# Chunks of 512 tokens in place of 384 in an attention + feed-forward kernel, with part of the second weight fetched from DRAM for each chunk

## Chip, cores and metric

One core of a Trainium2 chip. The time is device microseconds, the median of three runs: 662.34 us before (661.67 to 663.45).

## What is computed

Attention of 4 sequences of 768 tokens with 8 heads of 64. A query sees the keys within 16 tokens, and one summary per block of 32 tokens (maximum of its keys, mean of its values, log 32 added to its score). The output, 3072 tokens of 512, goes through two products with a gate between them, all in fp32:

```python
k_sum = k.reshape(B, H, nb, block, D).max(axis=3)
v_sum = v.reshape(B, H, nb, block, D).mean(axis=3)
mask_l = np.abs(pos[:, None] - pos[None, :]) < window
scores_all = concatenate([where(mask_l, scores_l, -1e9), scores_s + log(block)])
x = softmax(scores_all) @ concatenate([v, v_sum])      # 3072 x 512
h = x @ w_in                                           # 512 x 2048
sp = np.maximum(h, 0.0) + np.log1p(np.exp(-np.abs(h)))
g = h * erf(sp)
out = g @ w_out                                        # 2048 x 512
```

The weights come as 64-bit floats.

## The kernel before

**Chunks and periods.** The 3072 tokens are cut into NCH = 8 chunks of T = 384 (half a sequence each). For each chunk the 2048 inner columns are taken in NG = 4 groups of 512; a chunk's group is a *period* k, 32 in all. A *quad* is the attention of one chunk for two heads; a chunk has four, 32 in all, numbered so that quads 0 to 3 belong to the first chunk. The steady loop does one quad's attention in each period, a chunk ahead.

**First product** (`mm1`, L535 to L547). Weights and x are each split in two fp32r parts, high and low, and three products of parts are added: for each of four column tiles f (128 inner columns), 4 x 3 matmuls of 128 x 384 into one PSUM bank, `h0` or `h1` in turn. `hout` (L549) then reads the bank twice: ACT's tanh into `wt`, DVE's (early on also ACT's) copy into `hc`. `wt` and `hc` have three buffers each. `logs` and `erfs` (L564, L570) finish the gate on ACT; tanh and erf are in one table set, ln and exp in the other, and a table load (L780) is issued at each change. `gsplit` (L575) multiplies and splits on DVE.

**Second product** (`mm2`, L597) of period k-1 runs in period k: four tiles i times three token tiles t, accumulated over a chunk's four periods in banks `o0` to `o2`. For the first chunk it is plain fp32 on the unsplit weights (L605), later three fp32r matmuls of 512 columns (L609). `evac` (L618) copies the banks out at the end of a chunk.

**Attention.** `scores` (L419) into the double bank `pa`; `softmax` (L454) adds the mask (L457), takes the maximum (L465) and divides (L482) on DVE, exponentials on ACT one window at a time (L470); `transp` (L484) turns the result through `pa`, ACT copies it; `av` (L500) writes the output into a bank of its own, `px`; `xsplit` (L515) splits it into the parts xh and xl (L525). k, v and q windows come by DMA (`load_quad`, `load_quad_v`), their tiles single-buffered. `load_nat` and `summaries` (L324, L334) make a new sequence's summaries, starting four quads before its first chunk; `summaries_turn` transposes them through `px`.

**Weights.** Sixteen units of 1 MB, `load_w` (L237), in the order of `order` (L224). `convert` (L252) makes fp32 of the doubles' bits in three DVE steps, and for w_in the high and low part (ACT and DVE). `parts` (L291) splits w_out later, in periods 4 to 7. Slots w0 to w7 keep w_in's parts, w8 to w14 and the tiles a6 and a7 keep w_out's, all for the rest of the kernel.

**Order of the work.** Every operation is put on a list with its engine's estimated time (`Plan`, L45), what it reads and writes and so its dependencies. `due` gives due times by the list's order on PE; `order` (L91) then plays the list through, each engine taking the ready operation that is due first, and issues in that order. PE may take operations up to 60 places ahead among the first 330, and keeps the list's order after (L770). DMAs are all on SP's queue, in the planned order. Until the first write of `o2`, planned gaps on PE are filled with `busy` matmuls (L644, L774 to L778).

Of the kernel before, what the change touches and what calls it, by code (L numbers as in the profile page):

```python
# [21 lines left out]
NP = H // 2  # L22
NTH = 2
T = S // NTH
# [6 lines left out]
NCH = B * NTH  # L31
# [3 lines left out]
NQ = NCH * NP  # L35
WARM = 20
# [126 lines left out]
def block_attention_mlp(ctx: ExitStack, tc: tile.TileContext, q_t, k_nat, k_win, v_tok, v_nat, v_win, w_in, w_out, out):  # L163
# [3 lines left out]
    psum = ctx.enter_context(tc.tile_pool(name="ps", bufs=1, space=PSUM))  # L167
    ctx.enter_context(tc.manual_schedule())
# [12 lines left out]
    mask_sb = sb([128, 4, NK], F32, "mask_sb")  # L181
    nc.gpsimd.memset(mask_sb[:, :, 0:LW], 0.0)
    nc.gpsimd.memset(mask_sb[:, :, LW:NK], 8.0 * math.log(32.0))
    for c in range(2):
        m = mask_sb[64 * c:64 * c + 64, :, 0:LW]
        nc.gpsimd.affine_select(out=m, in_=m, pattern=[[0, 4], [1, LW]], compare_op=ALU.is_ge, fill=-8e9, base=-1, channel_multiplier=-1)
        nc.gpsimd.affine_select(out=m, in_=m, pattern=[[0, 4], [-1, LW]], compare_op=ALU.is_ge, fill=-8e9, base=31, channel_multiplier=1)
    nc.gpsimd.memset(mask_sb[0:64, 0, 0:16], -8e9)
    nc.gpsimd.memset(mask_sb[64:128, 3, 80:LW], -8e9)
# [4 lines left out]
    ksum = sb([128, NP, NS], F32, "ksum")  # L194
# [29 lines left out]
    order = [("i", 0), ("i", 1), ("o", 0), ("i", 2), ("o", 1), ("i", 3), ("o", 2), ("o", 3)]  # L224
    units = [(kind, g, r) for kind, g in order for r in range(2)]
    tiles, raws, whl, w32 = {}, {}, {}, {}
# [7 lines left out]
    def raw_slot(u):  # L234
        return number(u) if u[0] == "i" else 8 + number(u) % 4
# [14 lines left out]
    wide = {}  # L250

    def convert(u, home=None):  # L252

        w, s, m = f"w{raw_slot(u)}", {}, number(u)
        if u[0] == "o":
            home = f"a{m}"

        def a():
            if u[0] == "i" or m >= 6:
                s["t"] = sb([128, 2, 512], F32, "a32", home)  # L260
                if u[0] == "o":
                    w32[u] = s["t"]
            else:
                if m % 2 == 0:
                    wide[m // 2] = slot(12 + m // 2, [128, 2, 2, 512], F32, "a32s")
                s["t"] = w32[u] = wide[m // 2][:, m % 2]
            s["a"], s["rw"] = s["t"].bitcast(U32), raws.pop(u)
            nc.vector.tensor_scalar(s["a"], s["rw"][..., 1], 3, 0x3FFFFFFF, op0=ALU.logical_shift_left, op1=ALU.bitwise_and)
# [7 lines left out]
        def high():  # L276
            t = slot(raw_slot(u), [128, 2, 2, 512], F32R, "w")
            whl[u] = t[:, 0], t[:, 1]
            nc.scalar.copy(whl[u][0], s["t"])

        def low(e):
            e.tensor_tensor(whl[u][1], s["t"], f32(whl[u][0]), op=ALU.subtract)  # L282

        on({"DVE": 0.69}, lambda e: a(), [w], [home] + ([f"a{m + 1}"] if u[0] == "o" and m in (0, 2, 4) else []))
        on({"DVE": 1.22}, lambda e: b(), [w, home], [home])
        on({"DVE": 1.22}, lambda e: c(), [w, home], [home])
        if u[0] == "i":
            act(1.05, high, [home], [w])
            on({"DVE": 1.22}, low, [home], [w])

    def parts(u):  # L291

        m = number(u)
        n, home = 8 + m, f"a{m}"
        frees = [f"a{2 * (n - 12)}", f"a{2 * (n - 12) + 1}"] if 12 <= n < 15 else []
        if m < 7:
            def high():
                t = slot(n, [128, 2, 2, 512], F32R, "w")
                whl[u] = t[:, 0], t[:, 1]
                nc.scalar.copy(whl[u][0], w32[u])  # L300

            def low(e):
                e.tensor_tensor(whl[u][1], w32.pop(u), f32(whl[u][0]), op=ALU.subtract)
            act(1.05, high, [home], [f"w{n}"] + frees)
            on({"DVE": 1.22}, low, [home, f"w{n}"], [f"w{n}"])
            return

        def high():
            whl[u] = [sb([128, 2, 512], F32R, "wh", "a6")]
            nc.scalar.copy(whl[u][0], w32[u])  # L310

        def low(e):
            tiles["t1"] = sb([128, 2, 512], F32R, "wl", "t1")
            e.tensor_tensor(tiles["t1"], w32.pop(u), f32(whl[u][0]), op=ALU.subtract)

        def move(e):
            whl[u].append(sb([128, 2, 512], F32R, "wl", "a7"))
            copy(e, whl[u][1], tiles["t1"])
        act(1.05, high, ["a7"], ["a6"])
        on({"DVE": 1.22}, low, ["a6", "a7"], ["t1"])  # L320
        on({"DVE": 0.75}, move, ["t1"], ["a7"])
# [12 lines left out]
    def summaries(p):  # L334
        on({"DVE": 0.95}, lambda e: e.tensor_reduce(ksum[:, p], groups(tiles["t0"]), op=ALU.max, axis=AX.X), ["t0"], [f"ksum{p}"])
        on({"DVE": 0.95}, lambda e: e.tensor_reduce(vs_sum[:, LW:NK], groups(tiles["t1"]), op=ALU.add, axis=AX.X), ["t1"], ["vs_sum"])

    def summaries_turn(p):
        def go():
            tp = tiles["px"] = ps("px", "px")  # L340
            nc.tensor.transpose(tp[0:NK, 0:128], vs_sum, ident)  # L341
        pe(0.3, go, ["vs_sum"], ["px"])
        act(0.3, lambda: nc.scalar.mul(vsum[LW:NK, p], tiles["px"][LW:NK, 0:128], 1.0 / 32.0), ["px"], [f"vsum{p}"])


    V_SLOTS, K_SLOTS, Q_SLOT, P_SLOTS, W_SLOTS = (12, 4), (5, 6), 7, (13, 10), (14, 11)
# [9 lines left out]
    def where(qd):  # L356
        ch, p = divmod(qd, NP)
        b, th = divmod(ch, NTH)
        return ch, b, th, p

    def names(qd):

        if qd >= NP:
            return "qb", "kw", "pr", "vw", "vw"
        return f"w{Q_SLOT}", f"w{K_SLOTS[qd // 2]}", f"w{P_SLOTS[qd // 2]}", f"vwf{qd}", f"vwg{qd}"

    def load_qk_first(p):
        st[p] = dict(qb=qfs[:, p], vw=vws[p // 2][:, p % 2])
        dma(393, lambda: nc.sync.dma_start(out=kfirst[p], in_=k_nat[0, p]), w=[f"kf{p}"])
        dma(197, lambda: nc.sync.dma_start(out=qfs[:, p], in_=q_t[0, p, :, 0:T]), w=[f"qf{p}"])  # L370
# [5 lines left out]
    def load_vw_first(p):  # L376
        dma(295, lambda: nc.sync.dma_start(out=st[p]["vw"][0:LW], in_=v_win[0, p, 0]), w=[f"vwf{p}"])

    def ksum_first(p):
        on({"DVE": 0.95}, lambda e: e.tensor_reduce(ksum[:, p], groups(kfirst[p]), op=ALU.max, axis=AX.X), [f"kf{p}"], [f"ksum{p}"])  # L380

    def vsum_first(bank):
# [6 lines left out]
        act(0.65, lambda: nc.scalar.copy(vsum[LW:NK], tiles[bank][LW:NK].rearrange("s (p c) -> s p c", p=NP)), [bank], [f"vsum{p}" for p in range(NP)])  # L389
        for p in range(NP):  # L390
            on({"POOL": 0.9}, lambda e, p=p: e.tensor_copy(st[p]["vw"][LW:NK], vsum[LW:NK, p:p + 1, :].to_broadcast([NS, NB, 128])), [f"vsum{p}"], [f"vwg{p}"])


    def load_quad(qd):
        ch, b, th, p = where(qd)
        s = st[qd] = {}

        def go_q():
            s["qb"] = sb([128, T], F32, "qb")
            nc.sync.dma_start(out=s["qb"], in_=q_t[b, p, :, th * T:(th + 1) * T])  # L400

        def go_k():
            s["kw"] = sb([128, NB, NK], F32, "kw")
            nc.sync.dma_start(out=s["kw"], in_=k_win[b, p, th])
        dma(197, go_q, w=["qb"])
        dma(369, go_k, w=["kw"])
        on({"POOL": 0.35}, lambda e: e.tensor_copy(s["kw"][:, :, LW:NK], ksum[:, p:p + 1, :].to_broadcast([128, NB, NS])), [f"ksum{p}"], ["kw"])  # L407

    def load_quad_v(qd):
        ch, b, th, p = where(qd)  # L410
        s = st[qd]

        def go():
            s["vw"] = sb([NK, NB, 128], F32, "vw")
            nc.sync.dma_start(out=s["vw"][0:LW], in_=v_win[b, p, th])
        dma(295, go, w=["vw"])
        dma(80, lambda: nc.sync.dma_start(out=s["vw"][LW:NK], in_=vsum[LW:NK, p:p + 1, :].to_broadcast([NS, NB, 128])), [f"vsum{p}"], ["vw"])

    def scores(qd, banks=("pa",)):  # L419
# [3 lines left out]
        def go():  # L423
# [4 lines left out]
            for i in range(NI):  # L428
                for c in range(2):
                    j = 2 * i + c  # L430
                    for a in range(2):
# [3 lines left out]
                        else:  # L435
# [3 lines left out]
                            parts.append((LW, ksum[r, qd]))  # L439
# [3 lines left out]
        if qd >= NP:  # L443
            pe(0.8, go, ["qb", "kw"], banks)
        else:
            pe(1.1, go, [f"qf{qd}", f"kf{qd}", f"ksum{qd}"], banks)

    def softmax(qd, banks=("pa",)):
        ch, b, th, p = where(qd)
        s = st[qd]  # L450
        mk = mask_sb[:, th:th + NI]
# [24 lines left out]
        on({"DVE": 0.92}, add, banks, [pr])  # L476
        on({"DVE": 0.9}, red, [pr], [f"mx{par}"])
        on({"DVE": 0.17}, lambda e: e.tensor_scalar(s["mx"], s["mx"], -0.125, None, op0=ALU.mult), [f"mx{par}"], [f"mx{par}"])  # L478
        s["exps"] = act(2.45, exps, [f"mx{par}"], [pr, f"sm{par}"], table="log")
        on({"DVE": 0.17}, plus, [f"sm{par}"], [f"rs{par}"])  # L480
        on({"DVE": 0.19}, lambda e: e.reciprocal(s["rs"], s["rs"]), [f"rs{par}"], [f"rs{par}"])
        on({"DVE": 0.91}, lambda e: e.tensor_tensor(s["pr"], s["pr"], s["rs"].unsqueeze(2).to_broadcast([128, NB, NK]), op=ALU.mult), [f"rs{par}"], [pr])  # L482

    def transp(qd):  # L484
# [12 lines left out]
        pe(0.62, go, [pr], ["pa"])  # L497
        act(0.82, cp, ["pa"], ["pt"])

    def av(qd):  # L500
        s = st[qd]

        def go():
            xo = tiles["px"] = ps("px", "px")
# [5 lines left out]
        pe(0.88, go, ["pt", "vw"] if qd >= NP else ["pt", f"vwf{qd}", f"vwg{qd}"], ["px"])  # L510
# [4 lines left out]
    def xsplit(qd, eng):  # L515
        ch, b, th, p = where(qd)
        n = qd % NX

        def high(e):
            xt[ch, p] = [sb([128, T], F32R, m, f"{m}{n}") for m in ("xh", "xl")]  # L520
            copy(e, xt[ch, p][0], tiles["px"][:, 0:T])

        def low(e):
            st.pop(qd)
            e.tensor_tensor(xt[ch, p][1], tiles["px"][:, 0:T], f32(xt[ch, p][0]), op=ALU.subtract)  # L525
        on(eng, high, ["px"], [f"xh{n}"])
        on({"DVE": 0.56}, low, ["px", f"xh{n}"], [f"xl{n}"])
# [3 lines left out]

    def hbank(k, f):
        return f"o{f - 2}" if k == 0 and f >= 2 else f"h{f % 2}"
# [284 lines left out]
```

## Time and profile before

| | us |
|---|---|
| median of 3 runs | 662.34 |
| profiled execution, its own time | 661.75 |
| its span | 660.0 |
| PE busy | 653.7 |
| ACT busy | 473.1 |
| DVE busy | 414.9 |

The span is the profiled part of the execution, 1.75 us less than its time. Busy times overlap, so they don't add up to it; what sets the end is read from the chain of waits, followed back from the last instruction. The granted clock of TensorE is 1.000 over the whole span, the upper of its two levels.

### The profile page before, as it was taken

What the parts mean: (1) busy time and instruction counts of PE and PEld (TensorE: products, weight loads), DVE (VectorE), ACT (ScalarE), POOL (GpSimd) and SP (SyncE); (2) the same over time, 40 slices, a digit from 0 to 9 for tenths busy, and PEclk for the clock granted to TensorE, in tenths of its full rate; (3) what the DMA queues carried; (4) which work ended last, traced back from release to release, by engine and by line L of the source; (5) the groups of instructions that cost most, each with busy time, mean ns of one, the idle gap of its engine ahead of it and who ended that gap; (6) DMA issues with size and microseconds to landing.
All of it is one profiled execution on the core that took longest, in us unless ns stands there. A gap on an engine that the chain in (4) does not pass through costs nothing.

```text
span 660.0 us, 11458 instructions
## 1 busy us (share of the span) xinstructions
PE 653.7 (99%) x4600; PEld 554.5 (84%) x4600; DVE 414.9 (63%) x644; ACT 473.1 (72%) x871; POOL 19.8 (3%) x51
## 2 busy tenths in 40 slices
PE   9999999999999999999999999999999999999997
PEld 4677667778889999888999988899998889999996
DVE  4999899877555666655555576555556555544443
ACT  2669779887787776688766767877666877657662
POOL 2200000000000000000000000000000000000000
PEclk9999999999999999999999999999999999999999
DMA  9999743121121432222110443212011220001001
GB/s 329 301 314 355 247 148 124 54 79 58 58 58 58 157 113 69 73 89 74 58 47 14 151 130 105 81 58 91 18 56 59 89 73 23 1 1 49 0 1 48
DMA packets 29716, 64.50 MB, mean 98 GB/s; under 512 B 2976, under 2 KB 11872, under 8 KB 29664
## 3 DMA queue, kind: packets, MB, share of 16 engines
q1 hardware_dynamic: 29232, 63.39, 29.9%
q8 instruction: 36, 0.59, 0.4%
q10 hardware_dynamic: 432, 0.39, 0.2%
q14 instruction: 16, 0.13, 0.1%
HBM read 55.41 MB, written 6.29 MB: 93 GB/s over the span
## 4 chain that ended last, share of the span: by engine, by line
PE 92%; DMA 5%; DVE 1%; ACT 1%; SPq 0%; issue 0%
PE h L544 40%; PE ops L609 36%; PE ops L605 6%; PE px L509 4%; PE pa L442 3%; PE pa L492 3%; DMA rw<-w_in 2%; DMA vwf<-v_win 2%; DMA kf<-k_nat 1%; PE idle L647 1%; DVE a L271 0%; ACT pr L470 0%; PE px L341 0%; ACT L780 0%; DVE a L274 0%; DVE w L282 0%
## 5 line engine op out<-in xcount | busy, mean ns | idle before, releaser
L544 PE MATMUL h<-xh,w 128*128 128x384 f32 x1008 | 272.5, 341 | 0.4 <-ACT wt L555 0.4
L609 PE MATMUL ops<-w,gh 128*128 128x512 f32 x588 | 189.5, 396 | 0.0
L544 PEld LDWEIGHTS h<-xh,w 128*128 128x128 f32 x1008 | 183.9, 188 | 3.6 <-issue 0.9
L544 PE MATMUL h<-xl,w 128*128 128x384 f32 x504 | 170.0, 337 | 0.0
L780 ACT ACT_TABLE_LOAD x127 | 162.9, 1283 | 2.2
L555 ACT ACTIVATE wt<-h 128x384 f32<-128x384 f32 x126 | 61.1, 491 | 132.7 <-PE h L544 104.8
L219 DVE COPY hc<-h 128x384 f32<-128x384 f32 x117 | 65.2, 557 | 122.7 <-PE h L544 86.6
L609 PEld LDWEIGHTS ops<-w,gh 128*128 128x128 f32 x588 | 110.4, 188 | 25.0
L609 PE MATMUL ops<-w,gl 128*128 128x512 f32 x294 | 115.0, 391 | 0.0
L544 PEld LDWEIGHTS h<-xl,w 128*128 128x128 f32 x504 | 94.7, 188 | 2.2 <-issue 0.7
L470 ACT ACTIVATE pr<-pr,mx 128x120 f32<-128x120 f32 x168 | 64.1, 383 | 11.8 <-DVE mx L478 11.8
L585 DVE TENSOR_TENSOR hc<-wt,hc 128x768 f32<-128x768 f32 x56 | 51.7, 955 | 24.8 <-ACT wt L573 24.8
L609 PEld LDWEIGHTS ops<-w,gl 128*128 128x128 f32 x294 | 55.2, 188 | 11.1
L568 ACT ACTIVATE wt<-wt,half_b 128x768 f32<-128x768 f32 x64 | 60.1, 938 | 0.8
L592 DVE TENSOR_TENSOR gl<-hc,gh 128x768 fp32r<-128x768 f32 x56 | 53.1, 952 | 0.4
L573 ACT ACTIVATE wt<-wt 128x768 f32<-128x768 f32 x64 | 51.3, 839 | 0.4
L219 DVE CAST gh<-hc 128x768 fp32r<-128x768 f32 x56 | 29.2, 555 | 13.4 <-PE ops L609 13.3
L474 DVE TENSOR_SCALAR rs<-sm 128x6 f32<-128x6 f32 x32 | 5.6, 174 | 48.0 <-ACT pr L470 47.3
L605 PE MATMUL ops<-a32s,gw 128*128 128x512 f32 x72 | 31.9, 596 | 0.0
L470 ACT ACTIVATION_READ_ACCUMULATOR pr<-pr,mx 128x1 f32 x168 | 31.4, 187 | 0.0
L457 DVE TENSOR_TENSOR pr<-pa,mask_sb 128x720 f32<-128x720 f32 x28 | 25.4, 906 | 5.2 <-PE pa L442 5.2
L407 POOL COPY kw<-ksum 128x144 f32<-128x144 f32 x28 | 11.6, 416 | 503.9 <-DMA kw<-k_win 425.3
(103 smaller groups left out, 625.1 us busy)
## 6 DMA issues: line engine op xcount, KB each, us to landing
kw<-k_win SPq DMA_DIRECT2D x28, 360.0 KB
rw<-w_in SPq DMA_DIRECT2D x8, 1024.0 KB
rw<-w_out SPq DMA_DIRECT2D x8, 1024.0 KB
vw<-v_win SPq DMA_DIRECT2D x28, 288.0 KB
qb<-q_t SPq DMA_DIRECT2D x28, 192.0 KB
out<-ob SPq DMA_DIRECT2D x21, 256.0 KB
kvn<-v_nat SPq DMA_DIRECT2D x12, 384.0 KB
kvn<-k_nat SPq DMA_DIRECT2D x12, 384.0 KB
```

The costliest lines, as they stand in the source:

```text
L219: e.copy(o, i) if e is nc.scalar else e.tensor_copy(o, i)
L470: nc.scalar.activation(s["pr"][:, j], s["pr"][:, j], AF.Exp, scale=0.125, bias=s["mx"][:, j:j + 1], accum_out=sm[:, j:j + 1])
L509: nc.tensor.matmul(xo[r, o], lhsT=s["vw"][:, j, r], rhs=s["pt"][:, a, o], start=True, stop=True)
L544: nc.tensor.matmul(hs[k, f][:, 0:T], lhsT=w[m], rhs=xt[ch, cc][x], start=(cc == 0 and n == 0), stop=(cc == 3 and n == 2))
L555: nc.scalar.activation(wt[k, f // 2][:, f % 2], hs[k, f][:, 0:T], AF.Tanh, scale=0.5)
L568: act(0.86, lambda n=n: nc.scalar.activation(wt[k, n], wt[k, n], AF.Ln, scale=-0.49999994, bias=half_b), [s], [s], table="log")
L573: act(0.8, lambda n=n: nc.scalar.activation(wt[k, n], wt[k, n], AF.Erf, scale=-1.0), [s], [s], table="sig", after=after)
L585: e.tensor_tensor(hc[k, n], wt.pop((k, n)), hc[k, n], op=ALU.mult)
L592: e.tensor_tensor(gs[k, n][1], hc.pop((k, n)), f32(gs[k, n][0]), op=ALU.subtract)
L605: nc.tensor.matmul(os_[ch, t], lhsT=x[0][:, i % 2, t * 128:(t + 1) * 128], rhs=w32["o", g, i // 2][:, i % 2], start=first, stop=last)
L609: nc.tensor.matmul(os_[ch, t], lhsT=x[y][:, i % 2, t * 128:(t + 1) * 128], rhs=w[m], start=first and n == 0, stop=last and n == 2)
L780: nc.scalar.preload_act_table_set(sets[o["load"]])
```

## The change

T becomes 512: six chunks, 24 periods, 24 quads of eight windows. A chunk may now straddle two sequences, so k and v summaries of two sequences are kept at once (`ksum` and `vsum` by b % 2), POOL's and SP's copies of them are made per sequence, the mask has seven entries, and the new sequence's summaries start at quads 4, 12 and 16. The host lays out q_t, k_win and v_win by chunk.

PSUM: the second product takes a fourth bank `o3`; `px` is gone, and the attention output and the summaries' transposes take `h0` or `h1` in turn with the first product (`bank_next`), or `o2` at the beginning. `wt` and `hc` have two buffers instead of three.

SBUF: w_out's raw units use two slots (12, 13) instead of four. Parts 4 to 7 are split in period 3, written to DRAM (`put`), and read again for each later chunk (`get`) into slots 9 and 10, parts 4 and 5 after the second product in a chunk's first period, 6 and 7 in its last. Parts 0 to 3 are split in period 4 and stay.

The second chunk's attention, of which scores and softmax of the first quad and the loads of the second were issued ahead of period 0, is spread over periods 0 to 3 by hand (`early_att`).

```diff
-NTH = 2
-T = S // NTH
+T = 512
+SB = S // 64
...
-NCH = B * NTH
+NCH = B * S // T
...
+    WHOLE = {0: 11, 1: 10, 2: 8, 3: 9}
+    HOME = {0: 12, 1: 13, 2: 11, 3: 8, 4: 9, 5: 10, 6: 9, 7: 10}
+    kept = {}
...
     def raw_slot(u):
-        return number(u) if u[0] == "i" else 8 + number(u) % 4
+        return number(u) if u[0] == "i" else 12 + u[2]
...
+    def put(m, n):
+        u = ("o", m // 2, m % 2)
+
+        def go():
+            dr[m] = dram.tile([128, 2, 2, 512], F32, name=f"dr{m}", tag=f"dr{m}")
+            nc.sync.dma_start(out=dr[m], in_=f32(kept[u]))
+        dma(1049, go, [f"w{n}"], [f"d{m}"])
+
+    def get(m):
+        u, n = ("o", m // 2, m % 2), HOME[m]
+
+        def go():
+            t = slot(n, [128, 2, 2, 512], F32R, "w")
+            whl[u] = t[:, 0], t[:, 1]
+            nc.sync.dma_start(out=f32(t), in_=dr[m])
+        dma(1049, go, [f"d{m}"], frees(n))
...
+    turned = [0]
+
+    def bank_next():
+
+        turned[0] ^= 1
+        return f"h{turned[0]}"
+
+    def av(qd, bank):
         s = st[qd]
+        s["bank"] = bank
 
         def go():
-            xo = tiles["px"] = ps("px", "px")
+            xo = s["xo"] = ps("px", bank)
...
+    hbanks = {(0, 0): "h0", (0, 1): "h1", (0, 2): "o0", (0, 3): "o1"}
+
     def hbank(k, f):
-        return f"o{f - 2}" if k == 0 and f >= 2 else f"h{f % 2}"
+        if (k, f) not in hbanks:
+            hbanks[k, f] = bank_next()
+        return hbanks[k, f]
...
     def hout(k, f, eng):
-        bank, s = hbank(k, f), (2 * k + f // 2) % 3
+        bank, s = hbank(k, f), f // 2
...
-    load_quad(NP)
-    scores(NP)
-    softmax(NP)
-    load_quad(NP + 1)
-    load_quad_v(NP)
+
+    new = {1: 4, 2: 12, 3: 16}
...
+    def attend(n):
+
+        scores(n)
+        softmax(n)
+        load_quad_v(n)
+
+    def output(n, bank=None):
+        transp(n)
+        av(n, bank or bank_next())
+        xsplit(n, xeng)
+
+    def follow(n, bank=None):
+        sums(n, bank)
+        load_quad(n)
+        with_quad(load_nat, n + 1)
+
+    with_quad(load_nat, NP)
+    for u in units[4:6]:
+        load_w(u)
...
+    early_att = {(0, 3): [(lambda n: follow(n, "o2"), 4)], (1, 1): [(attend, 4), (lambda n: follow(n, "o2"), 5)],
+                 (1, 3): [(output, 4), (attend, 5), (follow, 6)], (2, 3): [(output, 5), (attend, 6), (follow, 7)],
+                 (3, 1): [(output, 6), (attend, 7), (follow, 8)], (3, 3): [(output, 7), (attend, 8), (follow, 9)]}
...
+        if k == 3:
+            for m in range(4, 8):
+                parts(m, 12 + m % 2)
+                put(m, 12 + m % 2)
+        if k == 4:
+            for m in range(4):
+                parts(m, HOME[m])
+        if k < NG:
+            for f in range(G):
+                if k and f % 2 == 0:
+                    gsplit(k - 1, f // 2, mult, cast, sub)
+                if k:
+                    mm1(k, f)
+                hout(k, f, heng)
+                for what, n in early_att.get((k, f), []):
+                    what(n)
+        else:
...
+            for f in (2, 3):
                 mm1(k, f)
...
+            if qs < NQ:
+                scores(qs)
+            if qa < NQ:
+                av(qa, bank_next())
...
         if k:
             mm2(k - 1)
+        if k >= NG and g in (0, 3):
+            for r in range(2):
+                get(6 + r if g else 4 + r)
         logs(k)
-        erfs(k, [st[qs]["exps"]] if qs < NQ else [])
+        erfs(k, [st[qs]["exps"]] if NG <= k and qs < NQ else [])
```

What is left out: the planner's costs, scaled to 512 tokens; the layouts; `sums` and `with_quad`, which issue a new sequence's summaries (their transposes in the steady loop come right behind the attention output); and the slots that the first attention borrows.

## Rows read from the trace of the kernel before

**Rows 1.** The page, busy time of each engine (us, share of the span, instructions).
```profile
PE 653.7 (99%) x4600; PEld 554.5 (84%) x4600; DVE 414.9 (63%) x644; ACT 473.1 (72%) x871; POOL 19.8 (3%) x51
```

**Rows 2.** Chain in order of time (start us, us, what), PE-bound stretch.
```profile
160.06 4.16 PE h L544 x24
...
198.15 4.22 PE h L544 x24
202.37 0.66 PE pa L492 x6
...
207.23 0.78 PE pa L442 x24
208.01 0.85 PE px L509 x24
208.86 8.52 PE ops L609 x36
...
227.27 0.85 PE px L509 x24
...
332.84 4.19 PE h L544 x24
```

**Rows 3.** The same chain, its start and its end.
```profile
48.92 1.32 PE h L544 x6
...
60.09 3.68 PE idle L647 x17
...
87.52 10.50 PE ops L605 x24
...
640.00 16.50 PE ops L609 x72
```

**Rows 4.** The page, GB/s of DMA in 40 equal slices of the span.
```profile
GB/s 329 301 314 355 247 148 124 54 79 58 58 58 58 157 113 69 73 89 74 58 47 14 151 130 105 81 58 91 18 56 59 89 73 23 1 1 49 0 1 48
```

**Rows 5.** Windows: sum, then busy us of PE, PEld, DVE, ACT, POOL; clock, DMA share, GB/s.
```profile
20.00:40.00 20.00, 19.02 (x226) 13.88 (x225) 18.62 (x29) 10.44 (x32) 3.31 (x4) 1.00 0.97 296
40.00:60.00 20.00, 19.58 (x166) 16.07 (x165) 19.23 (x29) 17.67 (x42) 0.30 (x1) 1.00 1.00 356
100.00:120.00 20.00, 20.00 (x121) 13.74 (x120) 18.82 (x27) 18.95 (x34) 1.08 (x1) 1.00 0.30 93
200.00:220.00 20.00, 20.00 (x144) 17.90 (x143) 10.74 (x18) 15.16 (x29) 0.31 (x1) 1.00 0.23 74
```

**Rows 6.** Timeline of PE, 648 to 657 us: start us, us, line, operation.
```profile
648.26 0.39 PE L609 MATMUL ops<-w,gl 128*128 128x512 f32 x1
...
651.66 0.39 PE L609 MATMUL ops<-w,gl 128*128 128x512 f32 x1
...
652.12 0.39 PE L609 MATMUL ops<-wh,gh 128*128 128x512 f32 x1
...
656.08 0.40 PE L609 MATMUL ops<-wl,gh 128*128 128x512 f32 x1
```

**Rows 7.** Groups by form: line, engine, shapes, xcount | busy us, mean ns | idle before.
```profile
L780 ACT ACT_TABLE_LOAD x127 | 162.9, 1283 | 2.2
...
L470 ACT ACTIVATE pr<-pr,mx 128x120 f32<-128x120 f32 x168 | 64.1, 383 | 11.8 <-DVE mx L478 11.8
...
L482 DVE TENSOR_TENSOR pr<-pr,rs 128x720 f32<-128x720 f32 x28 | 25.4, 907 | 0.8
L457 DVE TENSOR_TENSOR pr<-pa,mask_sb 128x720 f32<-128x720 f32 x28 | 25.4, 906 | 5.2 <-PE pa L442 5.2
...
L465 DVE TENSOR_REDUCE mx<-pr 128x6 f32<-128x720 f32 x28 | 25.0, 893 | 0.0
...
L525 DVE TENSOR_TENSOR xl<-px,xh 128x384 fp32r<-128x384 f32 x32 | 17.6, 549 | 0.5 <-ACT xh L219 0.4
```

**Rows 8.** Timeline of ACT, 222 to 228 us: start us, us, line, operation.
```profile
225.09 1.28 ACT L780 ACT_TABLE_LOAD   x1
226.38 0.49 ACT L555 ACTIVATE wt<-h 128x384 f32<-128x384 f32 x1
```

More of the change, by code (lines that the diff above doesn't have):

```diff
@@ L274, in c @@
             nc.vector.scalar_tensor_tensor(s["a"], s["rw"][..., 1], 0xC0000000, s["a"], op0=ALU.bitwise_and, op1=ALU.bitwise_or)
[L276 to L284, printed above, removed]
+        on({"DVE": 0.69}, lambda e: a(), [w], [home] if u[0] == "i" or u[2] else frees(WHOLE[u[1]]))
         on({"DVE": 1.22}, lambda e: b(), [w, home], [home])
@@ L287, in convert @@
         if u[0] == "i":
[L288 to L310, printed above, removed]
-        def low(e):
[L313 to L321, printed above, removed]
@@ new lines, in convert, with split, high, parts @@
+            split(u, raw_slot(u), home, lambda: s["t"])
+    def split(u, n, home, whole):
+        def high(e):
+            t = slot(n, [128, 2, 2, 512], F32R, "w")
+            whl[u] = t[:, 0], t[:, 1]
+            kept[u] = t
+            copy(e, whl[u][0], whole())
+        def low(e):
+            e.tensor_tensor(whl[u][1], whole(), f32(whl[u][0]), op=ALU.subtract)
+        on({"ACT": 1.05}, high, [home], frees(n))
+        on({"DVE": 1.22}, low, [home, f"w{n}"], [f"w{n}"])
+    def parts(m, n):
+        u = ("o", m // 2, m % 2)
+        split(u, n, f"a{m}", lambda: w32[u])
@@ L357, in where @@
         ch, p = divmod(qd, NP)
[L358 to L365, printed above, removed]
+        seqs = {}
+        for j in range(NB):
+            seqs.setdefault((NB * ch + j) // SB, []).append(j)
+        return ch, p, [(b, slice(js[0], js[-1] + 1)) for b, js in seqs.items()]
     def load_qk_first(p):
@@ L540, in go @@
             if cc == 0:
-                hs[k, f] = tiles[bank] = ps(bank, bank)
+                hs[k, f] = ps("h", bank)
             w = [t[:, cc % 2, f * 128:(f + 1) * 128] for t in whl["i", g, cc // 2]]
@@ L560, in hcopy @@
             copy(e, hc[k, f // 2][:, f % 2], hs[k, f][:, 0:T])
-        act(0.5, tanh, [bank], [f"wt{s}"], table="sig")
+        act(0.61, tanh, [bank], [f"wt{s}"], table="sig")
         on(eng, hcopy, [bank], [f"hc{s}"])
@@ L656, in block_attention_mlp @@
         load_vw_first(p)
-    for u in units[:6]:
+    for u in units[:4]:
         load_w(u)
@@ L715, in block_attention_mlp @@
         for u in loads.get(k, []):
             load_w(u)
-        if NG <= k < 2 * NG:
-            for r in range(2):
-                parts(("o", k - NG, r))
-        if k:
+        if k == 3:
[15 more added lines that the diff above has]
+        else:
+            gsplit(k - 1, 0, mult, cast, sub)
@@ L774, in block_attention_mlp @@
         if o["on"] == "PE":
-            filling = filling and "o2" not in o["w"]
+            filling = filling and "o3" not in o["w"]
             if filling:
```

255 lines of the change are left out of this document (127 added, 128 removed).

## The prediction

> **What bounds the kernel now.** I read the page first: PE is busy for 653.7 of 660.0 us [rows 1], so no other engine's total can matter unless it makes PE wait. PE's busy share doesn't say whether PE does needed work, so next comes the chain of waits in order of time. From 160.06 to 332.84 us it holds nothing but PE: nine periods in 172.78 us, 19.20 us each, and one of them shows the parts [rows 2]: two runs of 24 first-product matmuls (4.22 us), 6 transposes (0.66), scores (0.78), attention output (0.85), 36 second-product matmuls (8.52). Here a microsecond on ACT or DVE is worth nothing and one on PE is worth all of itself. Then the ends of the chain [rows 3]: the second period's first product begins at 48.92 us; 3.68 us of filler matmuls follow at 60.09, the only idle time of note behind that point; the second product of the first chunk, in plain fp32, takes 10.50 us a period; PE ends at 640.00 + 16.50 = 656.5. Before 48.92 the cover is different: DMA runs at 329, 301, 314, 355 GB/s in the first four slices [rows 4], and DVE is busy for 18.62 and 19.23 of each 20 us, still 18.82 in 100 to 120 [rows 5]. So: a start limited by DMA and DVE, then a PE stream of 607.6 us.
>
> The profiled execution took 661.75 us; the median is 662.34, 0.59 above. The sum is made against the former, and 0.6 is added at the end.
>
> **First product at 512 columns.** 24 matmuls of 384 columns take 4.16 to 4.22 us [rows 2], 4.20 in the middle, 175 ns a step. What a step of 512 costs shows in the second product, which already moves 512 columns: from 648.26 to 651.66 us fifteen steps take 3.40 us, 226.7 ns; from 652.12 to 656.08, on the tiles wh and wl, seventeen take 3.96, 233 ns [rows 6]. 233.3 is also 4/3 of 175, that is, no gain from longer matmuls. So the bounds are 226.7 and 233.3; I take 229, because 36 steps in 8.52 us less about 0.3 us to enter the run make 228, the nearest row, and the first product's steps scatter a little more. A period's first product is then 48 x 0.229 + 0.04 = 11.03 us in place of 8.40. Behind the 48.92 mark stand 31 periods of it before and 23 after: 260.4 against 253.7, **-6.7 us**. The bounds move this by -2.5 and +4.7.
>
> In a sentence of its own: the Trainium skill, "TensorE: Matmul & The Clock Gate", section "Back-to-back issue gap", gives N/2.4 + 2.5 ns at full clock, 162.5 and 215.8 ns here; the rows have 175 and 227 to 233, so the trace doesn't agree. By that rule the fixed part of a matmul is too small for longer ones to help, the term would be 23 x 10.36 - 31 x 7.80 = -3.5 us, and the sum 3.2 us worse.
>
> **Second product.** The fp32 chunk grows from 384 to 512 tokens: four periods of 10.50 x 4/3 = 14.0 us in place of 10.50, +14.0. The other 28 runs take 19.20 - 8.40 - 2.29 = 8.51 us with the gaps between the parts, and become 20 of 8.51 + 12 x 0.229 = 11.26: 238.3 to 225.2, -13.1. Together **+0.9 us**: a third more tokens go through the dearer fp32 form.
>
> **Attention on PE.** Per quad 2.29 us [rows 2]. Eight windows for six: transposes 0.66 x 8/6 = 0.88, scores and output a little less than in proportion, as each begins with an entry gap; I take 2.95 in all (3.05 in proportion, 2.29 + 2 x 0.3 = 2.89 if the gap is a third of them). Before, 28 quads less the scores of the second attention's first quad, which lay ahead of the mark: 63.3; after, 20 x 2.95 = 59.0: **-4.3 us**. The summaries' transposes stay twelve.
>
> **Work on other engines.** Table loads (127 of 1.28 us [rows 7], about four a period, for 32 and then 24 periods), tanh, logarithm, erf and softmax cost nothing in the PE-bound stretch: per 20 us ACT is busy for 15.16 and DVE for 10.74 at 200 to 220 [rows 5], and per token neither grows. If that cover went, each would cost its full duration, 0.49 to 1.28 us [rows 8].
>
> **The start.** The first attention now covers a third more tokens: per quad DVE's add, maximum, division and low part (906, 893, 907, 549 ns [rows 7]) gain a third, 1.09 us, less what is fixed, say 0.8; four quads +3.3 us. The first loads grow by 4 x (64 + 96) KB = 640 KB by the shapes in the code, 2.0 us at 330 GB/s. Against that the second attention's first quad leaves: four transfers of 360 + 192 + 288 + 72 = 912 KB on SP's queue ahead of the later weights, 2.7 us of DVE (add, maximum, division), and its exponentials on ACT (six steps of 0.38 us [rows 7]), which sat just ahead of the tanh that released PE. What goes and what comes nearly cancel. Bounds: -2.0 (the quad's leaving counts alone, with PE's part longer) and +5.3 (only the growth counts); I take **+1.1 us**, the last first-product pass being 12 x 54 ns longer plus half a microsecond of DVE, since DVE is the fuller queue.
>
> **Idle time in periods 0 to 3.** Now 3.7 us. Three things change. The wt and hc buffers go from three to two, so the tanh of period 1 must wait until period 0's product has been formed: a chain of tanh, load, logarithm, load, erf and multiplication on ACT and DVE, with no second product between to hide it. Queued behind that tanh are all of ACT's queue, and on PE the third first-product run of period 1, which needs the bank. Second, the new chunk straddles two sequences, so the next sequence's key and value loads (8 x 384 KB) and reductions are wanted a period earlier, on the SP queue among the weights and on the full DVE. Third, in favour, the period is a third longer for the same weight conversions. The bounds are 0 and 10 us (the 5.5 us of that chain twice, less what other work covers); I take 5.0, nearest to what the trace shows: **+1.3 us**.
>
> **Parts through DRAM.** Four writes of 1 MB once and four reads of 1 MB per chunk for five chunks, all on SP's queue behind the k, q and v loads: 3.2 us each at 330 GB/s. The reads of a pair may begin when half of a second product is done and are needed one period's first product and attention later, about 5.6 + 11 + 3 us. DMA then moves 47 to 159 GB/s in most slices [rows 4]. Cost nothing; with the cover gone, about 6 us a chunk, 30 us. The single-buffered kw load waits for scores already and stays as it is.
>
> **Attention output in h0 and h1.** A bank that was its own is now shared; what could wait is treated as the third rival. Cost nothing: from the end of the second run PE has 0.88 + 2 x 2.75 + 0.99 = 7.4 us before the output wants the bank; ACT must do tanh, load, logarithm, copy, load, tanh, 6.0 us at the new size.
>
> **Sum**: -6.7 + 0.9 - 4.3 + 1.1 + 1.3 = -7.7; 661.75 - 7.7 = 654.05, on the median's footing 654.65 us; I put 654.5. The tail (656.5 to the end) is unchanged.
>
> **Rivals.** (1) **512 columns cost in proportion.** For it: the wh and wl rows at 233 [rows 6], and the Trainium skill's gap rule above, which leaves longer matmuls next to nothing. Against: the 226.7 row. Price: +4.7 us in the first product, and if all 20 second products run at 233, 20 x 48 x 4 ns = +3.9: 659 to 663, say 661. Chance 0.15. (2) **The early periods don't fit DVE**: the weights' conversions, the earlier reductions and the wider softmax fill it beyond 20 of 20 us, and PE waits before the second and third period. For it: 18.82 of 20 at 100 to 120 us [rows 5]. Against: a period of 25 to 28 us in place of 21. Price: another 5 us of idle time, 660. Chance 0.10. (3) **Slower: PE waits for a shared h bank in each period.** Place: the attention output needs the bank of the third first-product run, whose tanh comes behind a table load. Before, that load began at 225.09, the tanh at 226.38, ended at 226.87, and the output began at 227.27 [rows 2, 8]: 0.40 us to spare, harmless then since the output had its own bank. By my count the margin becomes 1.4 us. The rival decides from the point where ACT comes later than that, by one more load for instance. Price: a load of 1.28 us less 0.4, 0.9 us in 20 periods, +18: 672 us. Chance 0.15. (4) **The DRAM reads arrive late** (a blocked SP queue): +6 us a chunk, 685 us; 0.03. The forecast has the remaining 0.57.
>
> **How the numbers follow.** The forecast's own range is 647 (226.7 ns everywhere, no idle time, start not later) to 659. To hold 8 in 10 it reaches over the first two rivals to 664; rivals 3 and 4 are left out above. A measurement of this kernel can tell about 0.3%, 2 us: faster means below 660.4, slower above 664.3. Faster: the forecast's 0.57, half of rival 2 (0.05), a third of rival 1 (0.05) and 0.03 of rival 3, where its price is small: 0.70. Same: the rest of rivals 1 and 2 without 0.03 of their far ends, 0.12. Slower: those 0.03, rival 3's other 0.12, rival 4: 0.18.
>
> **What would show it.** Right: first-product runs of 24 at 5.4 to 5.6 us, second products of 48 at 11.1 to 11.3, a period near 25.2 us, 24 x 4 table loads or fewer, no PE wait on h behind 80 us, second period's first product near 50 us. Wrong: "PE px" or "PE h" waiting on tanh or hc copies in each period (rival 3); ops waiting on a DMA (4); DVE at 20 of 20 and fillers after 75 us (2); steps of 233 ns (1).

## The result and the profile after

The changed kernel takes 664.98 us in the median (660.96 to 667.33, 20 runs), the one before 661.90 (660.93 to 663.45, 20 runs): a ratio of 1.0041, 95% interval 1.0026 to 1.0055. It is slower by 0.4%, where 654.5 was forecast. The profiled execution took 664.91 us with a span of 663.1.

The page of the changed kernel, busy time of each engine, answers to [rows 1]:

```profile
PE 652.9 (98%) x4216; PEld 497.7 (75%) x4224; DVE 399.6 (60%) x507; ACT 430.0 (65%) x770; POOL 27.1 (4%) x52
```

PE is busy almost throughout, as before, so the loss is in what PE does or in the little that it waits. The chain of waits in order of time (start us, us, what), one steady period and the end, answers to [rows 2, 3]:

```profile
203.20 5.57 PE h L563 x24
208.77 0.87 PE pa L499 x8
209.64 5.58 PE h L563 x24
215.22 0.98 PE pa L449 x32
216.21 1.08 PE px L524 x32
217.29 0.26 PE vt L345
217.54 11.14 PE ops L628 x48
...
637.30 22.30 PE ops L628 x96
```

Nothing but PE stands in the period. The transposes, scores and output take 2.93 us (2.95 forecast), the second product 11.14 (11.26), but the two runs of the first product 11.15 where 11.03 was forecast, and from 228.69 to 509.10 us eleven periods take 25.49 us each, not 25.24. In these, 0.26 us is a transpose of a new sequence's summaries (vt).

The start, in PE's timeline (start us, us, line, operation, in brackets the idle time before and what ended it): the first matmuls of the four passes of the first product in period 0 (one pass for each quad), the first matmul of period 1, and the only gap behind it.

```profile
30.61 0.48 PE L563 MATMUL h<-xh,w 128*128 128x512 f32 x1
...
37.77 0.59 PE L563 MATMUL h<-xh,w 128*128 128x512 f32 x1
...
43.73 0.58 PE L563 MATMUL h<-xh,w 128*128 128x512 f32 x1
...
50.30 0.58 PE L563 MATMUL h<-xh,w 128*128 128x512 f32 x1
...
54.55 0.50 PE L563 MATMUL h<-xh,w 128*128 128x512 f32 x1
...
60.74 2.54 PE L666 MATMUL idle<-zeros 128*128 128x512 bf16 x11
65.93 6.23 PE L624 MATMUL ops<-a32s,gw 128*128 128x512 f32 x10 [2.65 <-DVE a32s L283]
```

In the same view of the kernel before, the four passes begin at 28.68, 33.06, 38.92 and 43.43 us. Period 1 begins at 54.55 us, 5.6 later than before [rows 3]. The gap of 2.54 us of fillers and 2.65 us without any ends with ten matmuls in 6.23 us. The windows of that stretch (from:to, us, then busy us of PE, PEld, DVE, ACT, POOL, granted clock, DMA share, GB/s; the form of [rows 5]) say why:

```profile
54.00:60.00 6.00, 6.00 (x48) 4.60 (x40) 4.30 (x7) 5.25 (x7) 0.00 (x0) 1.00 0.90 332
60.00:66.00 6.00, 3.30 (x16) 1.55 (x15) 6.00 (x8) 5.95 (x20) 1.57 (x2) 1.00 0.77 282
66.00:72.00 6.00, 6.00 (x11) 2.48 (x12) 6.00 (x9) 5.93 (x7) 0.00 (x0) 0.72 0.83 282
72.00:78.00 6.00, 6.00 (x30) 4.67 (x29) 4.52 (x5) 3.13 (x6) 0.00 (x0) 1.00 0.46 175
```

After the stretch without matmuls the granted clock is 0.72 over 66 to 72 us, that is, part of it ran at the lower level of 1.2 GHz; twenty-two such matmuls at 108.92 us in the chain take 9.64 us, so ten at full clock would be 4.4 and the dip cost 1.85 us. DVE, on which PE waited, had itself stood for two loads:

```profile
53.45 0.70 DVE L277 TENSOR_SCALAR a<-rw 128x1024 uint32<-128x1024 uint32 x1 [1.36 <-DMA rw<-w_in]
...
57.04 0.95 DVE L338 TENSOR_REDUCE vs_sum<-kvn 128x24 f32<-128x768 f32 x1 [1.70 <-DMA kvn<-v_nat]
```

The chain shows which of these sets the end of the gap. It goes back from the matmuls at 65.93 us through DVE's work to the second load, a transfer for the new sequence's sums of v, and not through the beginning of period 1:

```profile
48.33 8.62 DMA kvn<-v_nat
...
64.65 1.15 DVE a32s L283
65.79 0.14 issue
65.93 6.23 PE ops L624 x10
```

**Where the 10.9 us between forecast and measurement lie** (664.91 against 654.05, both for a profiled execution): period 1 starts at 54.55 and not at 50.0, 4.5; then PE runs to 659.60, 605.05 us in place of 598.8, 6.3. Of these, the first product's steps are 232.7 ns in the mean (the distance of the starts of successive matmuls within a run) and not 229: 23 periods x 48 x 3.7 ns = 4.1; the dip 1.9; the idle time 5.2 in place of 5.0, 0.2. That leaves 0.1, and this is a balance: in the chain the summaries' transposes take about 2.6 us, for which the sum had no term of its own, and the second product and the attention together 2.3 less than their terms. The 4.5 us says where time lies and not what caused it: by the chain above, an earlier period 1 alone would have met a longer gap before 65.93 us.

### The profile page after: what moved, and what is told of

It reads as the page before. It is cut to its first block, busy times and chain, and to the rows that moved or that the text cites. A ratio compares the mean times of both kernels' runs of the same rounds, so it can differ in the third digit from the quotient of the medians.

```text
span 663.1 us, 10447 instructions
## 1 busy us (share of the span) xinstructions
PE 652.9 (98%) x4216; PEld 497.7 (75%) x4224; DVE 399.6 (60%) x507; ACT 430.0 (65%) x770; POOL 27.1 (4%) x52
## 4 chain that ended last, share of the span: by engine, by line
PE 90%; DVE 3%; DMA 3%; ACT 1%; SPq 1%; issue 0%; ACTq 0%; DVEq 0%
PE h L563 38%; PE ops L628 34%; PE ops L624 9%; PE px L524 4%; PE pa L499 3%; PE pa L449 3%; DMA kf<-k_nat 2%; DMA kvn<-v_nat 1%; DVE a L283 0%; ACT L825 0%; PE idle L666 0%; DVE w L299 0%; PE vt L345 0%; SPq L371 0%; DVE mx L472 0%
## 5 line engine op out<-in xcount | busy, mean ns | idle before, releaser
L563 PE MATMUL h<-xh,w 128*128 128x512 f32 x768 | 254.4, 402 | 0.0
L563 PEld LDWEIGHTS h<-xh,w 128*128 128x128 f32 x768 | 144.3, 188 | 36.3 <-issue 1.8
L574 ACT ACTIVATE wt<-h 128x512 f32<-128x512 f32 x96 | 57.1, 597 | 153.5 <-DVE hc L226 83.9
L563 PE MATMUL h<-xl,w 128*128 128x512 f32 x384 | 151.6, 395 | 0.0
L226 DVE COPY hc<-h 128x512 f32<-128x512 f32 x90 | 62.0, 690 | 134.1 <-PE h L563 122.5
L624 PE MATMUL ops<-a32s,gw 128*128 128x512 f32 x128 | 59.8, 611 | 2.7 <-DVE a32s L283 2.7
L604 DVE TENSOR_TENSOR hc<-wt,hc 128x1024 f32<-128x1024 f32 x40 | 47.7, 1222 | 16.8 <-ACT wt L592 16.5
L587 ACT ACTIVATE wt<-wt,half_b 128x1024 f32<-128x1024 f32 x48 | 55.3, 1152 | 0.6
L592 ACT ACTIVATE wt<-wt 128x1024 f32<-128x1024 f32 x48 | 49.2, 1054 | 0.3
L611 DVE TENSOR_TENSOR gl<-hc,gh 128x1024 fp32r<-128x1024 f32 x40 | 47.5, 1219 | 0.2
```

Of the source, the lines that this page charges most:

```text
L226: e.copy(o, i) if e is nc.scalar else e.tensor_copy(o, i)
L563: nc.tensor.matmul(hs[k, f][:, 0:T], lhsT=w[m], rhs=xt[ch, cc][x], start=(cc == 0 and n == 0), stop=(cc == 3 and n == 2))
L574: nc.scalar.activation(wt[k, f // 2][:, f % 2], hs[k, f][:, 0:T], AF.Tanh, scale=0.5)
L587: act(1.15, lambda n=n: nc.scalar.activation(wt[k, n], wt[k, n], AF.Ln, scale=-0.49999994, bias=half_b), [s], [s], table="log")
L592: act(1.05, lambda n=n: nc.scalar.activation(wt[k, n], wt[k, n], AF.Erf, scale=-1.0), [s], [s], table="sig", after=after)
L604: e.tensor_tensor(hc[k, n], wt.pop((k, n)), hc[k, n], op=ALU.mult)
```

## Experiments

Steps below are means of such distances of up to 0.3 us, from the trace's start times. Where a tile lies is read from the addresses that the program gives it: tiles are placed in the order of their first use, in steps of 32 bytes.

**1. Multiples of 128.** What differs between the 226.7 and the 233 ns of [rows 6] is where the tiles lie, gl, gh and the other w at multiples of 128 bytes, wh and wl not; the changed kernel's mask of 7 x 120 fp32 is 3,360 bytes, an odd number of 32-byte steps, and puts most tiles behind it off such multiples. So all sizes were rounded up to 128 bytes:

```diff
     def sb(shape, dtype, name, tag=None):
-        return pool.tile(shape, dtype, name=name, tag=tag or name)
+        n, e = math.prod(shape[1:]), 2 if dtype == BF16 else 4
+        ...
+        t = pool.tile([shape[0], -(-n * e // 128) * 128 // e], dtype, name=name, tag=tag or name)[:, 0:n]
```

> The changed kernel with every SBUF tile padded to a multiple of 128 bytes, so that each tile begins on a 128-byte boundary of its partition; nothing else differs. In the changed kernel nearly all large tiles begin 32 bytes off a 64-byte boundary (the mask grew to 3360 bytes, an odd number of 32-byte steps), and its 512-column steps take 232 to 233 ns. Theory A (where a tile begins sets the step): steps of the first and of the second product fall to about 227 ns, runs of 24 in the first product from 5.58 to 5.46 us, second products from 11.14-11.34 to about 10.95, a period from 25.49 to about 25.0, and the time from 665 to 653-656 us. Theory B (512 columns cost in proportion, whatever the place): steps stay at 232 to 233 and the time at 663 to 667.

Measured: 662.52 us (10 runs; ratio to before 0.9996, 0.9978 to 1.0013), steps of 230.9 and 231.3 ns in the first and second product: 2.5 us less than the changed kernel, and not 227 ns. The second edit adds a tile of 64 bytes in front of all of this:

> As the run with tiles padded to 128 bytes, but with a 64-byte tile ahead, so that every large tile begins 64 bytes off a 128-byte boundary. Theory A in its 64-byte form: as fast as the aligned one (653-656 us). Theory A in its 128-byte form, for which the kernel before speaks (its w_out tiles wh, wl, 64 bytes off, step at 233, those on a 128-byte boundary at 227): steps of 233 in both products, 663-667 us. Theory B: 663-667 us, no difference from the aligned run.

Measured: 663.56 us (1.0017, 1.0003 to 1.0032), the same steps, 230.9 and 231.2. So it isn't the multiple of 128 that counts.

**2. The kernel before, moved.** A tile of 32 bytes in front of everything:

```diff
+    nc.vector.memset(pool.tile([128, 8], F32, name="spacer", tag="spacer"), 0.0)
     ident = sb([128, 128], F32, "ident")
```

> The kernel before with a 32-byte tile ahead of all others, so that its large tiles, which began on 64-byte boundaries but for a few, begin 32 bytes off; nothing else differs. Theory A: its second product goes from 229 to about 232 ns a step (28 x 36 x 3 ns = 3 us) and its first product of 384 columns from 175 to 177-179 (31 x 48 x 3 ns = 4 us): 665 to 670 us. Theory B: 662 us as before.

Measured: 662.11 us (0.9997, 0.9988 to 1.0007), steps of 176.7 and 229.9 ns, to the tenth those of the kernel before. All tiles moved and nothing changed: the theory as it stood falls. What a common shift leaves as it is, is how tiles lie *to each other*.

Then the kernel before with kw, pr and the twelve small tiles of the softmax placed first, in one block:

```diff
+    for name, n in [("kw", 720), ("pr", 720)] + [(f"{m}{i}", 6) for m in ("mx", "sm", "rs") for i in range(4)]:
+        nc.vector.memset(sb([128, n], F32, name)[:, 0:1], 0.0)
     P = Plan()
```

> The kernel before with its small tiles and kw and pr placed first, so that every large tile that PE reads begins on a 128-byte boundary. Theory A: second product at 227 ns throughout (28 x 36 x 2.3 ns = 2.3 us), first product 173.5 in place of 175 (31 x 48 x 1.5 ns = 2.2 us): 657 to 659 us. Theory B: 662 us.

Measured: 658.67 us (0.9948, 0.9933 to 0.9963), steps of 175.8 and 227.9 ns. From one period in the chain, against [rows 2]:

```profile
197.51 4.19 PE h L547 x24
...
208.16 8.41 PE ops L612 x36
```

The second product is 8.41 us in this and in 21 more periods, where before it took 8.32 to 8.60. The time is in the range that the first theory gave, though the run above had refuted that theory. In this kernel all tiles that the two products read happen to begin at the same place modulo 512 bytes, 384; with sizes rounded to 128 alone the changed kernel's lie at 0, 128, 256 and 384.

**3. One place modulo 512.** In the changed kernel the small tiles, kw and pr go first too (every large tile is then a multiple of 512 bytes), and a spacer sets the common place:

```diff
+    for name, n in [("kw", 960), ("pr", 960)] + [(f"{m}{i}", 8) for m in ("mx", "sm", "rs") for i in range(4)] + [("spacer", 88)]:
+        nc.vector.memset(sb([128, n], F32, name)[:, 0:1], 0.0)
     P = Plan()
```

> The changed kernel, with the twelve small tiles of the softmax and kw and pr placed together ahead of the large tiles, so that every large tile begins at the same place modulo 512 bytes (384). Placement theory (what a matmul step costs depends on where the tiles that PE reads lie relative to each other modulo 512 bytes, and in the kernel before with all tiles at multiples of 128 they happened to lie so): steps of 226 to 228 ns in both products, 654 to 657 us. Rival (512 columns cost 4/3 of 384 whatever the placing, or the DRAM traffic slows the steps): steps of 229 to 233 ns as with multiples of 128 alone, 661 to 664 us.

> The same with every large tile at 0 modulo 512 bytes. If one common residue is enough: steps of 226 to 228 ns, 654 to 657 us, like the kernel at 384. If 384 is a place of its own and only the absolute address counts: 230 to 233 ns, 661 to 664 us.

> The same with every large tile at 32 modulo 512 bytes, no multiple of 64. If one common residue is all that counts: 226 to 228 ns, 654 to 657 us. If it takes multiples of 64 or 128 as well: 231 to 233 ns and 663 to 666 us, like the changed kernel.

Measured: 655.34 us at 384 (0.9878, 0.9836 to 0.9919), 654.51 at 0 (0.9886, 0.9861 to 0.9912), 655.71 at 32 (0.9901, 0.9885 to 0.9918), with 227.0 to 227.4 ns in both products of all three. One common place is enough, and which one doesn't matter, not even an odd multiple of 32. A period of the kernel at 384, in the chain:

```profile
197.51 5.44 PE h L566 x24
202.96 0.87 PE pa L502 x8
203.83 5.47 PE h L566 x24
209.30 0.98 PE pa L452 x32
210.28 1.08 PE px L527 x32
211.36 0.26 PE vt L348
211.62 10.92 PE ops L631 x48
```

**4. The counter-test.** The same kernel, with only gh and gl, the stationary tiles of the second product, 64 bytes further:

```diff
-            gs[k, n] = [sb([128, 2, T], F32R, m, f"{m}{n}") for m in ("gh", "gl")]
+            gs[k, n] = [sb([128, 2 * T + 128], F32R, m, f"{m}{n}")[:, 16:16 + 2 * T].rearrange("p (a b) -> p a b", a=2) for m in ("gh", "gl")]
```

> The changed kernel with all large tiles at 384 modulo 512 bytes but gh and gl, the stationary tiles of the second product, moved by 64 bytes. If a step costs more where the two tiles that PE reads lie differently modulo 512 bytes: second product's steps from 227 to 230 to 234 ns, first product's still 227, 3 to 7 us more (658 to 662). If only the placing of the small tiles counted: 227 in both, 654 to 656.

Measured: 661.15 us (0.9976, 0.9960 to 0.9992). First product 227.8 ns, second 233.3, by nothing but the place of its stationary tile. In the chain:

```profile
203.51 5.47 PE h L566 x24
...
217.64 11.19 PE ops L631 x48
```

The addresses and the start times together, second product, by the place of the moving tile less that of the stationary one, modulo 512 bytes:

```
kernel                     difference   steps   mean ns
before                          0        600     227.8
before                        192        358     233.3
changed                       128        528     232.4
changed                       224        160     229.5
changed                       256         76     234.6
changed                       352        120     233.6
changed                       480         40     229.2
changed, all at 0               0        924     227.3
changed, gh and gl + 64       448        924     233.3
```

The rows at 226.7 and 233 ns [rows 6] are the first two lines of this table. In the changed kernel no matmul of either product has difference 0. Between the kernels at mixed places the means follow no simple order (neighbouring matmuls of different places influence each other), so the table settles only that 0 is the cheapest, and even that needs the neighbour: in the second product of the kernel with sizes rounded to 128 bytes, steps with difference 0 take 227.3 ns where the next matmul has 0 too (260 steps), but 232.3 where it has 384 (268 steps). Odd and even multiples of 512 bytes between the two tiles give the same, 227.2 and 227.5 ns in the kernel at 0. With 384 columns no such order shows in the kernel before: the first product's steps behind 54 us take 177.0 ns at difference 0 and 175.2 at 192.

**5. The passes of period 0.** The attention output of a quad is listed ahead of the first product on the quad before it:

```diff
-    for p in range(NP):
-        transp(p)
-        av(p, "o2")
-        xsplit(p, {"DVE": 0.69, "ACT": 0.6})
-        for f in range(G):
-            mm1(0, f, (p,))
+    for p in range(NP + 1):
+        if p < NP:
+            transp(p)
+            av(p, "o2")
+            xsplit(p, {"DVE": 0.69, "ACT": 0.6})
+        for f in range(G if p else 0):
+            mm1(0, f, (p - 1,))
```

> The changed kernel, with one reordering in the first period: the attention output of a quad is listed ahead of the first product on the quad before it, so that PE has work while the output is split. Theory (the start is later by 5.6 us because each pass of the first product waits for a split that got longer): second period's first product at 49.5 to 51.5 instead of 54.55, 661 to 663 us, since part of it comes back as a wait behind it. Rival (DVE and ACT are full up to 100 us and set the end of period 1 anyway): the mark moves but the time stays at 664 to 666 us.

Measured: 663.82 us (1.0019, 0.9999 to 1.0039), against 664.98 a gain of 1.2 that the spread of both doesn't make certain. In its profile the four passes took 18.7 us (37.83 to 56.56) and not 23.9, as the theory says, but they began 7 us later, so the mark came at 56.56 and not at 49.5 to 51.5. Inconclusive by itself; what stood in front of them is the next point.

**6. PE waits for its instructions.** In the profiles of six of the kernels above, PE stands in the middle of one group, always behind the 25th of the 32 matmuls of the first attention output, for 3.3 to 4.8 us, for nothing that the profile shows ("issue"). PE's timeline of the kernel at 0 modulo 512:

```profile
23.36 0.97 PE L527 MATMUL px<-ptr,vwf 120*64 120x64 f32 x25
29.14 0.69 PE L527 MATMUL px<-ptr,vwf 120*64 120x64 f32 x7 [4.81 <-issue]
29.76 5.20 PE L669 MATMUL idle<-zeros 128*128 128x512 bf16 x17
```

The DMA view has a queue of kind "instruction". For the same kernel, 26 to 28 us (queue, kind: packets, MB, share of 16 engines):

```profile
q1 hardware_dynamic: 145, 0.54, 98.6%
q8 instruction: 1, 0.02, 3.8%
```

By the records these packets on q8 are 16 KB each. The one that matters runs at 26.70 us here and PE goes on behind it; in the kernel at 384, whose profiled execution took 650.16 us and shows no such wait, it runs at 20.40. The six with the wait have it at 25.0 to 26.9 us, the two without (that one, and the changed kernel with a wait of 0.2) at 20.4 and 21.3. The DMA engines that carry it are full of data (98.6% above). The kernel before has issued as many matmuls only at 32.3 us, here it is 24 us, since a third more of the small attention matmuls come first. After the wait the clock falls as well (windows of the kernel at 0):

```profile
26.00:28.00 2.00, 0.00 (x0) 0.00 (x0) 1.88 (x4) 0.00 (x0) 0.62 (x1) 1.00 1.02 277
28.00:30.00 2.00, 0.86 (x8) 0.63 (x9) 0.00 (x0) 0.13 (x1) 0.00 (x0) 0.78 1.01 342
30.00:32.00 2.00, 2.00 (x6) 0.73 (x5) 0.57 (x1) 1.40 (x2) 0.00 (x0) 0.50 1.07 334
```

0.50 is the lower level, 1.2 GHz, after 4.8 us without a matmul. To need fewer instructions there, the fillers were made longer: fp32, about a quarter as many in the program (24 for 88). In the trace each is two matmuls of 430 ns, where a bf16 one takes 216, so the engine's records of fillers fall from 88 to 48.

```diff
-WARM = 20
+WARM = 5
...
-    zeros = sb([128, 512], BF16, "zeros")
+    zeros = sb([128, 512], F32, "zeros")
...
-                busy(int(0.8 * (o["start"] - free_at) / 0.22))
+                busy(int(0.8 * (o["start"] - free_at) / 0.87 + 0.5))
```

> The changed kernel with all large tiles at 384 modulo 512 bytes, and its filler matmuls in fp32 (four passes each) in place of bf16, so a quarter as many: 26 instructions of TensorE fewer ahead of the first attention output. Theory (in most runs PE stands 3.3 to 4.8 us after the 348th matmul because its next 16 KB of instructions come late through the loaded DMA engines; with a third more attention matmuls in the start it needs them earlier than the kernel before did): no issue wait of over 1 us ahead of the first product, first product at 30 to 32 us, second period's at 54 to 56, 650 to 652 us in the median. Rival (the instructions are late by chance and the start is set by DVE and the loads): the median stays at 654 to 656 us.

Measured: 652.62 us (0.9852, 0.9838 to 0.9866), four runs from 651.72 to 653.08, a granted clock of 1.00 in each, where the kernels of point 3 had 0.994 to 0.999. No issue wait; the packet runs at 23.08. 2.7 us less than at 384 with short fillers, and the spread of 6 us there is gone (four runs each). The one execution at 384 with short fillers that is known to have had no wait, 650.16 us, was still faster, so the long fillers seem to cost something of their own. Period 1 starts at 57.34, later than the theory had it (the first product itself begins at 32.37), and the median lies 0.6 us above its range, 1.4 below the rival's. One profile shows the wait gone; that the whole gain comes from it is not shown.

> The kernel before with all large tiles at one place modulo 512 bytes, and with the fp32 fillers. Theory: it never stood for instructions, so nothing changes: 657.5 to 659.5 us, and with the changed kernel at 650 to 652 the change is worth 7 us (1.1%) on equal terms. Rival (fewer fillers help any kernel's start): 653 to 656 us.

Measured: 660.23 us (0.9968, 0.9956 to 0.9979), 1.6 more than with the short ones and 0.7 above the range named. The kernel before never stood for instructions and has nothing to win there; its first product begins at 29.95 us in place of 28.85, and why is not shown. On these equal terms, one place and long fillers in both, the change is worth 7.6 us (660.23 to 652.62).

> The same, with the attention output of a quad listed ahead of the first product on the quad before it. If the passes of the first period are held by the split of the attention output: second period's first product at 49 to 51 us, and 647 to 650 us. If what is won there comes back as a wait for ACT's tables behind it: 650 to 652 us, like the kernel without it.

Measured: 650.49 us (0.9824, 0.9809 to 0.9839), the best of all, 1.8% below the kernel before. The time lies in the second case's range, and the mark at 52.92 us is later than the first case had it. From PE's timeline, the first matmuls of periods 0 and 1:

```profile
34.09 0.50 PE L566 MATMUL h<-xh,w 128*128 128x512 f32 x1
...
52.92 0.50 PE L566 MATMUL h<-xh,w 128*128 128x512 f32 x1 [0.50 <-ACT wt L577]
```

18.8 us for the four passes, against 25.0 (32.37 to 57.34) without the reordering. Of the 4.4 us that period 1 starts earlier, 2.1 reach the end. The instructions are not wholly in time here either: in this profile PE stands 1.97 us for "issue" at 17.54 us, in the scores of the third quad.

## Why the prediction was wrong

**First product, the step that failed.** "I take 229": the forecast put the changed kernel between 226.7 and 233.3 by which row was nearest. Both ends were right, but what chooses between them was not chance or scatter but the place of the tiles, and the change moved it: 232.7 ns. Point by point, the rival "512 columns cost in proportion" named the measured step (233) and a price near the measured time, 661 us before the start's loss, but nearly half of that price, +3.9 us for the second products, did not come (11.14 to 11.34 us, 11.26 forecast), and its mechanism is wrong: with all tiles at one place the same 512 columns take 227.4 ns, 1.29 times the 175.8 of 384, so longer matmuls do gain. With each kernel's tiles at one place, the change takes the time from 658.67 to 654.51 us, -4.2, and with the long fillers in both from 660.23 to 652.62, -7.6, where -7.7 was forecast; the kernel before is better off with the short ones, and best against best is -6.0. That -7.6 is so near is in part luck: there period 1 begins at 57.34 us and not at 50.0, and the steps lie below the 229 ns of the forecast. As it was made, it gave about 10 us back through addresses.

**Second product.** 11.14 to 11.34 us a period against 11.26: right in size, because the row it came from, 36 steps in 8.52 us [rows 2], lies between the 8.41 of tiles at one place and the 8.60 that such a product takes at worst in the chain of before. Part of this is luck: the change moved its steps too, from 229.9 to 232.1 ns in the mean.

**Attention on PE.** 2.93 us a quad against 2.95: right.

**The start, the second step that failed.** +1.1 us was forecast as "the last first-product pass being 12 x 54 ns longer plus half a microsecond of DVE"; measured +5.6. The passes begin 1.9 us later, at 30.61 us, and take 23.9 us in all in place of 20.2. Each stands behind the split of the output of its own quad, which waits behind the pass before it: 7.2, 6.0, 6.6 and 4.3 us by the timeline above, before 4.4, 5.9, 4.5 and 5.5. So not the last pass grew but the first and the third, and the order holds them: with the outputs listed ahead the four take 18.7 and 18.8 us (points 5 and 6). How much of the 5.6 us reaches the end stays open, since the chain to 65.93 us goes through the load of v and DVE and not through period 1's start; 4.4 us won at the start were worth 2.1 at the end (point 6). Start and idle time together grew by 7.1 us, where 2.4 was forecast.

**Idle time.** 5.0 us forecast, 5.2 measured, and in the right place; that the clock would fall behind it, 1.9 us more, was not foreseen. The rival "the early periods don't fit DVE" is partly right: DVE is what PE waits for at 65.93, full from 60 to 72 us, but behind a load that landed at 56.95, and no fillers follow.

**Not foreseen at all** was the instruction queue. It cost next to nothing in the profiled execution of the changed kernel, a wait of 0.2 us, and 3 to 5 us in those of six relatives. Whether it makes the changed kernel's spread of 6 us is not shown: the granted clock is 0.999 and 1.00 in the two fastest runs (660.96 and 661.33 us) and 0.991 in the slowest (667.33), but three more with 1.00 lie at 662.92 to 664.59, and no profile of a slower run was taken.

**Right** were the DRAM parts (no wait for them in the chain), the shared banks (px follows the scores at once, 216.21 us; once in the span, at 546.79 us, it waited 0.21 us for a tanh, so the third rival was near and did not come), and the tables: 105 loads where 96 were expected and 127 were before, hidden.

```profile
L825 ACT ACT_TABLE_LOAD x105 | 134.7, 1283 | 1.9
```

## What to carry to other kernels

If matmuls of one shape show two step times in a trace, look up where their two operands lie before taking a mean: place all tiles that TensorE reads at one address modulo 512 bytes (sizes in multiples of 512, small tiles in one block in front) and compare again. A change of a tile's size moves all that is allocated behind it, so a comparison of two kernels should be made with like placing. Where a start is full of small matmuls while the DMA engines are full of loads, look for "issue" waits at a fixed instruction, and if there are any, try fillers that are longer and fewer; without such a wait they cost 1.6 us here.

## What the runs showed of the hardware that was not expected

A step of 512 fp32r columns takes 227 ns where moving and stationary tile begin at the same place modulo 512 bytes, in the next matmul too, and 229 to 235 elsewhere in the mean by place; with 384 columns the median is 173 ns with all at one place, and 174 without. 64 bytes on one operand are 6 ns a matmul, 5.8 us in this kernel. The Trainium skill, "SBUF — State Buffer", section "SBUF: two separate sides", has TensorE's ports wait for nobody, and gives the weights a read port of their own; the trace disagrees in so far as a step depends on how the two tiles lie, 233.3 against 227.3 ns. That TensorE's two reads hinder each other is a likely reason, which no run shows by itself.

TensorE's instructions are fetched while the kernel runs, 16 KB at a time, through the DMA engines that carry the data, and in one profile PE stood 4.8 us for them. The profile page of the changed kernel lists 33 packets on that queue, 0.54 MB, which over PE's 8,440 matmuls and weight loads is 64 bytes each; in the kernel before 36 packets go with 9,200, again 64 each. That this queue is TensorE's own is inferred from that and from the moments of the waits.

```profile
q8 instruction: 33, 0.54, 0.3%
```
